# A linear-attention and feed-forward kernel: the engines' order written by hand, and the weights loaded in order through one queue

## The chip, the cores and the metric

The kernel runs on one core of one Trainium2 chip. The metric is device time in microseconds (us) of one execution. Each number called a time is the median of two to eleven executions. All executions of all kernels here were in the fast state, on several chips of the same kind, so each variant is set against executions of the kernel before on the same chip, in the same rounds. A ratio is the mean time of one kernel's fast runs over the mean time of the other's fast runs of the same rounds, so it is not quite the ratio of the medians that are quoted.

The profile covers one execution. It measures a span, which is a little shorter than the time; the profiled execution of the kernel before has a span of 220.7 us.

Engines: PE is TensorE (matmul), PEld its weight loads, DVE is VectorE, ACT is ScalarE, POOL is GpSimd, SP is SyncE, which here only issues transfers (SPq in the profile).

## The reference

Two layers follow each other. The first is a linear attention with a decay `f` per channel, with 4 batches, 8 heads, 768 tokens and a head width of 48. The second is a feed-forward network with a leaky ReLU, from 384 to 2048 and back, over all 3072 tokens.

```python
f = 1.0 / (1.0 + np.exp(-f_logit))
for t in range(S):
    state = f[:, :, t, :, None] * state + einsum('bhd,bhe->bhde', k[:, :, t], v[:, :, t])
    y[:, :, t] = einsum('bhd,bhde->bhe', q[:, :, t], state)
x = y.transpose(0, 2, 1, 3).reshape(B * S, H * D)     # 3072 x 384
h = x @ w_in                                          # 384 -> 2048
out = np.maximum(0.01 * h, h) @ w_out                 # 2048 -> 384
```

Inputs and outputs are float32. Both kernels compute the products in bf16.

## The kernel before

The work is cut into 24 units: 6 chunks of 128 tokens for each of 4 batches. The four batches of a chunk come first, then the next chunk. A unit has an attention part and a feed-forward (FFN) part, and the FFN of a unit stands two units behind its attention in the source. The order of the instructions on each engine is not that of the source: a scheduler in the compiler chooses it.

Attention of one unit has these steps, with the tile names that the profile shows. Four loads bring `f_raw`, `q`, `k` (both into `qk_raw`) and `v_raw`. ACT makes `t_e` and `lf` (the logarithm of the decay). TensorE sums it over the tokens (`cs`), ACT takes two exponentials of that (`ex`), and DVE multiplies q and k with them (`qkh`, the decay product). TensorE transposes (`tp`), DVE copies (`qkT`), TensorE multiplies k with q on 64 rows (`pw`), DVE masks (`wm`), TensorE forms the output (`py`), DVE copies it (`xnat`), and a DMA transposes it (`xT`). On the side, `pt`, `a_e`, `a_d`, `st`, `sf` and `sb` carry the state to the next chunk.

```python
    inp = ctx.enter_context(tc.tile_pool(name="inp", bufs=4))
    ...
    def load_weights():
        for kk in range(3):
            nc.gpsimd.dma_start(out=w_in_b[:, kk, :],          # float32 to bf16 on the way
                                in_=moe_w_in[kk * 128:(kk + 1) * 128, :])
        for kk in range(4):
            nc.gpsimd.dma_start(out=w_out_b[:, 4 * kk:4 * kk + 4, :], in_=moe_w_out[...])

    def attn(u):
        ...
        nc.sync.dma_start(out=f_raw, in_=f_logit[b, :, ts, :].rearrange("h t d -> t h d"))
        ...                                                    # q, k, v in the same way
        if u == 0:
            load_weights()
        nc.scalar.activation(t_e, f_raw, AF.Exp, scale=-1.0)
        nc.scalar.activation(lf[:, :, 0:D], t_e, AF.Ln, bias=1.0)
        nc.gpsimd.tensor_copy(out=v_b, in_=v_raw)
        nc.tensor.matmul(cs, ut, lf[:, :, 0:D], start=True, stop=True)
        nc.scalar.activation(ex[:, 0:H, :], cs, AF.Exp, scale=-1.0)
        nc.scalar.activation(ex[:, H:2 * H, :], cs, AF.Exp, scale=1.0)
        nc.vector.tensor_mul(qkh[:, :, 0:D], qk_raw, ex)
        ...                                                    # tp, qkT, pw, wm, py, xnat
        nc.sync.dma_start_transpose(xT, xnat)
        ...                                                    # state for the next chunk
        return xT

    def ffn(u, xT):
        for g in range(4):                                     # 4 x 12 up products
            for j in range(4):
                for kk in range(3):
                    mm(pm[:, j, :], w_in_b[:, kk, ...], xT[:, kk, :], 3 * j + kk, 12)
            nc.scalar.activation(gT[:, 4 * g:4 * g + 4, :], pm, AF.Prelu, alpha=0.01)
        for ff in range(16):                                   # 16 down products
            mm(po, gT[:, ff, :], w_out_b[:, ff, :], ff, 16)
        nc.vector.tensor_copy(out=osb, in_=po)
        nc.sync.dma_start(out=out[...], in_=osb)

    waiting = []
    for u in range(NU):
        waiting.append((u, attn(u)))
        if len(waiting) > DEPTH:                               # DEPTH = 2
            ffn(*waiting.pop(0))
```

## Time and profile before

| | before |
|---|---|
| time, median of 3 | 221.88 us (221.37 to 223.13) |
| span of the profiled execution | 220.7 us |
| first up product of unit 0 | 36.04 us |
| first transposes of neighbouring units, steady | 7.575 us apart |

First come the span, the busy times and the row of TensorE on the page of the kernel before. Each digit of the row is the busy share of one fortieth of the span, in tenths.

```profile
span 220.7 us, 5773 instructions
...
PE 178.7 (81%) x2376; PEld 135.4 (61%) x2376; DVE 105.5 (48%) x149; ACT 98.7 (45%) x213; POOL 50.0 (23%) x100
...
PE   0000045999798989999999999999999999999993
```

TensorE is busy 81% of the span. The row shows where the rest is: at five and a half microseconds per digit, the first seven are empty or half empty. This is why the share of the whole span should not be read as a property of the steady part. The table of stretches separates the two. Its columns are the stretch, its length, the busy time and count of PE, PEld, DVE, ACT and POOL, the granted clock, the share of the DMA engines, and GB/s. The DMA share sums the time of packets in flight and can pass 1.

```profile
0.00:10.00 10.00, 0.48 (x1) 0.10 (x1) 0.83 (x9) 2.33 (x3) 5.88 (x16) 1.00 0.83 153
10.00:20.00 10.00, 0.00 (x0) 0.00 (x0) 0.00 (x0) 0.00 (x0) 0.00 (x0) 1.00 1.20 187
20.00:30.00 10.00, 1.64 (x16) 1.11 (x16) 1.65 (x2) 2.74 (x6) 1.01 (x2) 1.00 1.11 197
30.00:40.00 10.00, 5.34 (x62) 4.46 (x63) 4.70 (x7) 3.65 (x9) 4.22 (x8) 1.00 1.02 201
...
100.00:120.00 20.00, 19.64 (x268) 15.06 (x266) 11.13 (x17) 10.30 (x24) 4.22 (x10) 1.00 0.66 144
```

In the first 40 us TensorE works 7.5 us (0.48 + 0.00 + 1.64 + 5.34), and the DMA engines are full all along. In 100 to 120 us TensorE is busy 19.64 of 20 us. A reader could conclude that nothing is to be gained there. The chain of waits says otherwise. Its columns are start, duration and what ran, and the rows are those of one round in the steady part.

```profile
107.06 1.95 PE po L89 x12
109.01 0.18 PE cs L115
...
109.21 0.49 ACT ex L117
109.70 0.38 ACT ex L118
110.08 0.50 ACT gT L188
...
110.62 0.49 PE pm L89 x6
...
111.13 0.62 PE tp L89 x8
```

The records of matmuls overlap: that of an up product is 220 ns long in the mean on this kernel's page, while up products start 56 ns apart where nothing waits. So a TensorE that reads as busy can be one whose next instruction waits. On this chain a round leaves TensorE: `cs` releases the two `ex`, they hold up `gT` on ACT, and only then do the last 6 up products run. Three ACT instructions, 0.49 + 0.38 + 0.50 = 1.4 us, stand on the chain of nearly every steady round. Not all of that is lost, since TensorE works on meanwhile. The distance between matmul starts shows how much is: in the round from 111.13 us on, the step to the last 6 up products is 329 ns where up products otherwise start 56 ns apart, the step from an up product to the first transpose is 230 ns in place of 56, and the step from a down product to the `py` that needs the mask is 275 ns in place of 162. Together that is 0.27 + 0.17 + 0.11 = 0.56 us of waiting in the round.

Three rows of the timeline show the start of the same kernel. Columns are start, duration, engine, line, operation, tiles and shapes, and in brackets the idle time before with what ended it.

```profile
23.40 0.50 POOL L112 CAST v_b<-v_raw 128x384 bf16<-128x384 f32 x1 [16.95 <-DMA v_raw<-in_v_dram]
...
25.20 0.52 ACT L109 ACTIVATE t_e<-f_raw 128x384 f32<-128x384 f32 x1 [20.51 <-DMA f_raw<-in_f_logit_dram]
...
36.04 0.80 PE L89 MATMUL pm<-xT,w_in_b 128*128 128x128 bf16 x6 [1.63 <-DMA xT<-xnat]
```

Unit 0's `v` has landed only at 23.4 us, and unit 1's `f` at 25.2 us, though all the loads were issued from 0.74 us on. The weights, loaded on POOL's queue, shared the DMA engines with them.

### The profile page before, as it was taken

To read this page: it belongs to the slowest core of one execution; us is meant where nothing else is said; L and a number is where in the kernel's file an instruction comes from. 1 tells how busy PE (TensorE), PEld (TensorE's weight loads), DVE (VectorE), ACT (ScalarE), POOL (GpSimd) and SP (SyncE) were. 2 spreads that over 40 slices of the span, in tenths; PEclk is the share of its full clock that TensorE was granted. 3 is DMA by queue.
4 is the path that set the end of the run, shared out by engine and by line. 5 is a ranking of instruction groups with operands and counts; after the bars stand their busy time and mean duration, and the time that the engine had idled before them with its cause. 6 is when DMAs were issued, how large, how long until landed. Compare 5 with 4: busy or idle time off the path is not lost.

```text
span 220.7 us, 5773 instructions
## 1 busy us (share of the span) xinstructions
PE 178.7 (81%) x2376; PEld 135.4 (61%) x2376; DVE 105.5 (48%) x149; ACT 98.7 (45%) x213; POOL 50.0 (23%) x100
## 2 busy tenths in 40 slices
PE   0000045999798989999999999999999999999993
PEld 0000034777576777777778777767777777767771
DVE  1000144765655755574566467555745666356211
ACT  4000324753744665474556446553744462535440
POOL 8100115433203303321331133033213300000000
PEclk9999999999999999999999999999999999999999
DMA  6999999578979797986766675554724411011200
GB/s 112 203 186 184 199 198 201 109 147 179 215 165 198 173 197 155 229 179 151 160 142 150 139 146 125 120 134 80 157 61 88 110 53 56 18 39 53 56 36 36
DMA packets 115850, 29.46 MB, mean 133 GB/s; under 512 B 110321, under 2 KB 115441, under 8 KB 115825
## 3 DMA queue, kind: packets, MB, share of 16 engines
q1 hardware_dynamic: 113280, 25.96, 55.9%
q0 software_dynamic: 2544, 3.15, 8.3%
q8 instruction: 18, 0.29, 0.6%
q14 instruction: 8, 0.06, 0.1%
HBM read 25.17 MB, written 4.72 MB: 135 GB/s over the span
## 4 chain that ended last, share of the span: by engine, by line
PE 63%; ACT 14%; SPq 12%; DMA 6%; DVE 2%; issue 2%; DVEq 0%; ACTq 0%
PE po L89 26%; PE pm L89 18%; PE tp L89 6%; PE py L89 5%; ACT gT L188 5%; ACT ex L117 4%; DMA f_raw<-in_f_logit_dram 4%; SPq L101 4%; PE pw L89 3%; ACT ex L118 3%; SPq L98 3%; SPq L99 3%; SPq L100 3%; PE pt L89 2%; DVE wm L134 2%
## 5 line engine op out<-in xcount | busy, mean ns | idle before, releaser
L89 PE MATMUL pm<-xT,w_in_b 128*128 128x128 bf16 x1152 | 80.4, 220 | 6.6 <-ACT gT L188 3.0
L89 PEld LDWEIGHTS <-w_in_b 128*128 128x128 bf16 x1152 | 68.8, 98 | 14.8 <-issue 11.6
L89 PE MATMUL po<-w_out_b,gT 128*128 128x384 bf16 x384 | 69.9, 326 | 0.0
L188 ACT ACTIVATE gT<-pm 128x512 bf16<-128x512 f32 x96 | 56.4, 597 | 19.3 <-PE pm L89 17.8
L89 PEld LDWEIGHTS <-gT 128*128 128x128 bf16 x384 | 34.9, 97 | 19.1
L117 ACT ACTIVATE ex<-cs 128x384 bf16<-128x384 f32 x24 | 11.7, 490 | 47.1 <-PE cs L115 47.1
L193 DVE COPY osb<-po 128x384 f32<-128x384 f32 x24 | 13.4, 557 | 39.8 <-PE po L89 39.7
L134 DVE TENSOR_TENSOR wm<-pw,ut 128x1024 bf16<-128x1024 f32 x24 | 29.4, 1223 | 3.8 <-PE pw L89 3.1
L109 ACT ACTIVATE t_e<-f_raw 128x384 f32<-128x384 f32 x24 | 12.5, 522 | 33.8 <-DMA f_raw<-in_f_logit_dram 33.8
L125 DVE COPY qkT<-tp 128x1024 bf16<-128x1024 bf16 x24 | 16.6, 691 | 17.2 <-PE tp L89 17.2
L89 PE MATMUL tp<-ident,qkh_88 128*128 128x128 bf16 x64 | 5.4, 231 | 22.4 <-DVE qkh_88 L119 22.3
L112 POOL CAST v_b<-v_raw 128x384 bf16<-128x384 f32 x24 | 13.5, 561 | 40.3 <-DMA v_raw<-in_v_dram 23.0
L163 POOL TENSOR_TENSOR a_d<-a_e,half 128x8 f32<-128x8 f32 x20 | 4.0, 202 | 80.7 <-ACT a_e L161 80.7
L89 PEld LDWEIGHTS <-qkh_88 128*128 128x128 bf16 x92 | 5.5, 103 | 27.0 <-DVE qkh_88 L119 26.9
L119 DVE TENSOR_TENSOR qkh_88<-qk_raw,ex 128x768 bf16<-128x768 f32 x8 | 7.7, 956 | 27.8 <-ACT ex L118 27.8
L147 DVE CAST xnat<-py 128x384 bf16<-128x384 f32 x24 | 13.4, 557 | 11.0 <-PE py L89 10.5
L89 PEld LDWEIGHTS <-qkT 64*128 64x128 bf16 (+1 forms) x272 | 9.6, 97 | 6.5 <-DVE qkT L125 2.1
L89 PEld LDWEIGHTS <-wm 128*128 128x128 bf16 x192 | 6.6, 97 | 9.2 <-DVE wm L134 9.1
L118 ACT ACTIVATE ex<-cs 128x384 bf16<-128x384 f32 x24 | 11.7, 487 | 0.0
L89 PE MATMUL py<-v_b,wm 128*128 128x48 bf16 x192 | 9.1, 186 | 2.2 <-DVE wm L134 2.1
L119 DVE TENSOR_TENSOR qkh_92<-qk_raw,ex 128x768 bf16<-128x768 f32 x8 | 7.7, 958 | 6.5 <-ACT ex L118 6.5
L89 PE MATMUL pw<-qkT 64*128 64x128 bf16 x192 | 9.9, 226 | 0.8 <-DVE qkT L125 0.8
(60 smaller groups left out, 123.7 us busy)
## 6 DMA issues: line engine op xcount, KB each, us to landing
f_raw<-in_f_logit_dram SPq DMA_DIRECT2D x24, 192.0 KB, 3.4
qk_raw<-in_q_dram SPq DMA_DIRECT2D x24, 192.0 KB, 3.7
qk_raw<-in_k_dram SPq DMA_DIRECT2D x24, 192.0 KB, 3.9
v_raw<-in_v_dram SPq DMA_DIRECT2D x24, 192.0 KB, 3.5
out_dram<-osb SPq DMA_DIRECT2D x24, 192.0 KB, 2.1
w_in_b<-in_moe_w_in_dram POOLq DMA_DIRECT2D x3, 512.0 KB, 8.9
w_out_b<-in_moe_w_out_dram POOLq DMA_DIRECT2D x4, 384.0 KB, 16.1
xT<-xnat SPq DMA_TRANSPOSE x24, 2.8
```

The lines of the kernel that those rows point to most:

```text
L89: nc.tensor.matmul(o, l, r, start=(i == 0), stop=(i == n - 1), is_transpose=(True if tr else None))
L101: nc.sync.dma_start(out=v_raw, in_=v[b, :, ts, :].rearrange("h t d -> t h d"))
L109: nc.scalar.activation(t_e, f_raw, AF.Exp, scale=-1.0)
L112: nc.gpsimd.tensor_copy(out=v_b, in_=v_raw)
L117: nc.scalar.activation(ex[:, 0:H, :], cs, AF.Exp, scale=-1.0)
L118: nc.scalar.activation(ex[:, H:2 * H, :], cs, AF.Exp, scale=1.0)
L119: nc.vector.tensor_mul(qkh[:, :, 0:D], qk_raw, ex)
L125: nc.vector.tensor_copy(out=qkT, in_=tp)
L134: nc.vector.tensor_mul(wm, pw.rearrange("a r p t -> a (r p) t"), ut[:, None, :].to_broadcast([128, 2 * NP, 128]))
L147: nc.vector.tensor_copy(out=xnat, in_=py.rearrange("a h d -> a (h d)"))
L188: nc.scalar.activation(gT[:, 4 * g:4 * g + 4, :], pm, AF.Prelu, alpha=0.01)
L193: nc.vector.tensor_copy(out=osb, in_=po)
```

## The change

The intent is twofold. In the steady part every engine gets its order by hand, so that independent TensorE work stands between each producer and its consumer. At the start the loads arrive in the order in which they are needed. Four things change together:

- The source is turned into a loop over rounds in the order of the engines, and `manual_schedule` makes the compiler keep it. In one round the attention of unit i is interleaved with quarters of the FFN of unit i-2 and with the preparation of unit i+1.
- The weights are loaded as float32 quarters through SP's queue, behind and between the first units' loads, and POOL casts them.
- Units 0 and 1 are turned by TensorE (three transposes and a copy) instead of a DMA.
- `inp` gets a fifth buffer. `sb` is doubled, which the new order needs: a round writes the new state before it reads the old one.

```diff
-    inp = ctx.enter_context(tc.tile_pool(name="inp", bufs=4))
+    inp = ctx.enter_context(tc.tile_pool(name="inp", bufs=5))
...
-        sb = const.tile([128, NP, 2 * D], BF16, tag=f"sb{b}", name=f"sb{b}")
+        sb = [const.tile([128, NP, 2 * D], BF16, tag=f"sb{b}{i}", name=f"sb{b}{i}")
+              for i in range(2)]
...
-    def load_weights():                    # 7 casting loads on POOL's queue
...
+    def load_w_in(g):
+        t = wst.tile([128, 3, 512], FP32, tag=f"wi{g}", name=f"wi{g}")
+        nc.sync.dma_start(out=t, in_=w_in_v[:, :, 512 * g:512 * g + 512])
+        staged["i", g] = t
+    def cast_w_in(g):
+        nc.gpsimd.tensor_copy(out=w_in_b[:, :, 512 * g:512 * g + 512], in_=staged["i", g])
...                                         # load_w_out, cast_w_out in the same way
-        nc.sync.dma_start_transpose(xT, xnat)
+            if self.u < LAG:               # LAG = 2
+                for i in range(3):
+                    mm(tx[:, i, :], xnat[:, 128 * i:128 * i + 128], ident, i, 3, tr=True)
+                nc.vector.tensor_copy(out=self.xT, in_=tx)
+            else:
+                nc.sync.dma_start_transpose(self.xT, xnat)
...
-    waiting = []
-    for u in range(NU):
-        waiting.append((u, attn(u)))
-        if len(waiting) > DEPTH:
-            ffn(*waiting.pop(0))
-    for w in waiting:
-        ffn(*w)
+    ctx.enter_context(tc.manual_schedule())
...
+    units[0].load()
+    for g in range(4):
+        load_w_in(g)
+    units[1].load()
+    load_w_out(0)
+    load_w_out(1)
+    units[2].load()
+    load_w_out(2)
+    load_w_out(3)
+    units[0].prep()                        # t_e, lf, v_b
+    units[0].cumsum()                      # cs, ex
+    units[0].decay()                       # qkh
+    for g in range(4):
+        cast_w_in(g)
+    for i in range(NU + LAG):
+        a, n, m = unit(i), unit(i + 1), unit(i - LAG)
+        unit(i + 3).load()
+        m.up(0)
+        m.up(1)
+        a.transposes()                     # tp, qkT
+        a.update_state()                   # pt, a_e, a_d, st, sf, sb
+        n.prep()
+        if i == 1:
+            for g in range(4):
+                cast_w_out(g)
+        m.down(0)
+        m.up(2)
+        a.scores()                         # pw, py with the state, wm
+        m.down(1)
+        m.up(3)
+        n.cumsum()
+        a.outputs()                        # py with wm, xnat, xT
+        n.decay()
+        m.down(2)
+        m.down(3)
+        m.store()
```

## The prediction

> **What bounds the kernel now.**
>
> *Start.* In the table of stretches TensorE is busy 0.5, 0.0, 1.6 and 5.3 us in the first four 10 us, with the DMA engines at least 83% busy. The timeline shows why: the weights (casting loads on POOL's queue) share the 16 DMA engines with the first units' loads; v_raw of unit 0 lands at 23.4 us, unit 1's f_raw at 25.2. Unit 0's first up product runs at 36.0. That all queues run on the same 16 engines and interleave is what the Trainium skill says (DMA: Bandwidth & Descriptors, "Issuing engines are not separate DMA queues"); this trace agrees.
>
> *Steady state.* From 80 to 200 us TensorE is busy 97.8%; the first transpose of successive units comes every 7.575 us (88.40, 95.98, 103.55 in the chain of waits). But that busy time holds pipeline latency. The chain has 18 up products in 1.00 us (56 ns each) and 12 down products in 1.95 us (162 ns). 48 up (2.67) + 16 down (2.59) + 8 transposes (0.45) + cs 0.16 + pw 0.21 + py and state 0.37 + pt 0.27 make 6.7 us, with 0.12 at the change from the 64-row pw 6.85. So about 0.6 us per unit is wait: the chain passes through ACT (ex, ex, gT: 1.4 us per unit) before the last up products and the decay product, then qkT to pw, and wm to py.
>
> **What the change does.** Between cs and the next unit's transposes stand py, two down and two up quarters (2.9 us of TensorE), against 2.7 us for gT, ex, ex and decay (0.97 us): just hidden. qkT (0.69) hides behind pt, down and up (1.6), wm (1.22) behind down, up and cs (1.5). I expect 7.0 us per round (6.75 without pt in four), 5.3 in the two rounds without attention.
>
> Weights: fp32 through SP's queue, in order. 192-byte packets take 15.9 ns (mean of the records), so a unit's 4096 packets take 4.1 us on 16 engines. A weight quarter, estimated from the 65 ns of the 1536-byte output packets: 2.1 us. So unit 0 lands at 6.5 us, w_in at 15, unit 1 at 19, unit 2 at 27.5, w_out at 32, unit 3's f at 33. Added: eight POOL casts, estimated 2.0 us each from 503 ns per 384 columns. The w_out casts stand behind the cast of unit 2's v, end near 36 us and gate round 2, which ends at 36.7. Unit 2's DMA transpose stands behind the loads of units 4 and 5 (some 1 us).
>
> **Sum.** 36.7 + 17 x 7.0 + 4 x 6.75 + 2 x 5.3 + 1 + 3.4 (last product to end, as before) = 198; timed runs lie 1.2 us above the span: 199 us. Some 14 of the 23 us gained come from the start.
>
> Chances: faster by over 2% 0.96, within 2% 0.03, slower 0.01. Range 194 to 206.
>
> **What would show it.** First transposes every 7.0 us; no large ACT releaser before up products; TensorE near full from 37 us, with waits before that for POOL's w_out casts and f_raw; first up product near 27 us.
>
> **What would make it wrong.** Slower weight packets or POOL casts (10% is 2 us); an order on ACT or DVE that keeps a wait in each round (0.2 us is 4 us in all); a backlog on SP's queue that delays every transpose.

## The result and the profile after

| | before | after |
|---|---|---|
| time, median (4 runs each, same rounds) | 221.84 us | 201.17 us (200.44 to 201.67) |
| ratio, 95% interval | | 0.9057 (0.9009 to 0.9105) |
| span of the profiled execution | 220.7 us | 198.7 us |
| first up product of unit 0 / unit 8 / unit 23 | 36.04 / 101.43 / 211.63 us | 28.42 / 87.32 / 189.30 us |
| distance of the first transposes of neighbouring units, steady | 7.575 us | 6.967 us |

The changed kernel is faster by 9.4%. All outputs are right. The page of the kernel after has these busy times and this row of TensorE:

```profile
span 198.7 us, 5720 instructions
...
PE 171.8 (86%) x2382; PEld 137.4 (69%) x2382; DVE 106.1 (53%) x151; ACT 103.4 (52%) x213; POOL 55.8 (28%) x101
...
PE   0401449898999999999999999999999999999992
```

The table of stretches of the kernel after, for the same stretches:

```profile
0.00:10.00 10.00, 2.53 (x25) 1.91 (x26) 3.36 (x13) 3.37 (x6) 2.23 (x10) 1.00 0.82 211
10.00:20.00 10.00, 1.10 (x12) 0.73 (x11) 1.38 (x2) 1.92 (x4) 7.37 (x7) 1.00 0.99 284
20.00:30.00 10.00, 4.93 (x53) 4.17 (x52) 5.51 (x8) 2.15 (x6) 3.72 (x6) 1.00 1.06 298
30.00:40.00 10.00, 9.37 (x129) 7.49 (x127) 6.32 (x9) 5.61 (x13) 7.32 (x9) 1.00 1.02 235
...
100.00:120.00 20.00, 20.00 (x291) 16.12 (x287) 12.77 (x18) 12.56 (x27) 5.64 (x12) 1.00 0.73 154
```

In the first 40 us TensorE now works 17.9 us (2.53 + 1.10 + 4.93 + 9.37) instead of 7.5. In 100 to 120 us TensorE is busy 20.00 of 20 us. This time it is real: from 46 to 183 us no two matmuls start more than 0.17 us apart, and the longest steps are those behind 384-column products (0.16 us) and at `pw` (0.15 us). One round on the chain of waits:

```profile
106.72 0.16 PE cs L131
106.88 0.20 PE py L100 x8
107.08 1.30 PE po L100 x8
108.38 1.34 PE pm L100 x24
109.72 0.45 PE tp L100 x8
```

The chain now stays on TensorE. `cs`, `py`, 8 down products, 24 up products and the transposes follow each other at the pace of their starts (the 24 up products take 1.34 us, 56 ns each), with no ACT row between them. The start, in rows of the timeline that answer to those before, with some that are used further down:

```profile
6.26 1.10 POOL L127 CAST v_b<-v_raw 128x384 bf16<-128x384 f32 x1 [4.57 <-DMA v_raw<-in_v_dram]
...
28.42 2.56 PE L100 MATMUL pm<-xT,w_in_b 128*128 128x128 bf16 x24
...
28.94 2.11 DVE L138 TENSOR_TENSOR qkh_96<-qk_raw,ex 128x768 bf16<-128x768 f32 x1
...
30.18 2.19 POOL L97 CAST w_out_b<-wo_142 128x1536 bf16<-128x1536 f32 x1
...
34.45 0.53 ACT L124 ACTIVATE t_e<-f_raw 128x384 f32<-128x384 f32 x1 [2.27 <-DMA f_raw<-in_f_logit_dram]
...
35.58 0.32 PE L131 MATMUL cs<-lf_87,ut 128*128 128x384 bf16 x1 [0.51 <-ACT lf_87 L125]
```

Unit 0's `v` is cast at 6.26 us instead of 23.40, and the first up product starts at 28.42 us instead of 36.04. One wait in the steady part was left, the one for the first transpose by DMA, that of unit 2:

```profile
41.31 2.73 SPq L208 DMA_TRANSPOSE xT<-xnat  x1
...
45.51 1.51 PE L100 MATMUL pm<-xT,w_in_b 128*128 128x128 bf16 x24 [1.17 <-DMA xT<-xnat]
```

SP issues it at 41.31 us, and the up products that need it start at 45.51 us, after TensorE has waited 1.17 us.

### The profile page after: what moved, and what is told of

The parts are those of the page before. It is cut to its first block, busy times and chain, and to the rows that moved or that the text cites. A ratio compares the mean times of both kernels' runs of the same rounds, so it can differ in the third digit from the quotient of the medians.

```text
span 198.7 us, 5720 instructions
## 1 busy us (share of the span) xinstructions
PE 171.8 (86%) x2382; PEld 137.4 (69%) x2382; DVE 106.1 (53%) x151; ACT 103.4 (52%) x213; POOL 55.8 (28%) x101
## 4 chain that ended last, share of the span: by engine, by line
PE 78%; SPq 13%; DMA 6%; ACT 1%; issue 1%; DVE 0%; ACTq 0%
PE po L100 30%; PE pm L100 30%; SPq L120 10%; PE py L100 5%; PE tp L100 5%; DMA f_raw<-in_f_logit_dram 4%; PE pw L100 3%; PE pt L100 2%; DMA xT<-xnat 2%; PE cs L131 2%; SPq L85 1%; SPq L90 1%; ACT gT L219 0%; DVE osb L230 0%; ACT t_e L124 0%
## 5 line engine op out<-in xcount | busy, mean ns | idle before, releaser
L219 ACT ACTIVATE gT<-pm 128x512 bf16<-128x512 f32 x96 | 57.2, 597 | 64.3 <-PE pm L100 60.2
L100 PEld LDWEIGHTS <-w_in_b 128*128 128x128 bf16 x1152 | 71.3, 99 | 10.6 <-DMA xT<-xnat 1.6
L100 PE MATMUL pm<-xT,w_in_b 128*128 128x128 bf16 x1152 | 77.1, 221 | 1.2 <-DMA xT<-xnat 1.2
L100 PE MATMUL po<-w_out_b,gT 128*128 128x384 bf16 x384 | 74.5, 325 | 0.2
L100 PEld LDWEIGHTS <-gT 128*128 128x128 bf16 x384 | 32.4, 97 | 17.0 <-ACT gT L219 1.5
L100 PEld LDWEIGHTS <-wm 128*128 128x128 bf16 x192 | 8.6, 98 | 13.7 <-issue 11.8
L127 POOL CAST v_b<-v_raw 128x384 bf16<-128x384 f32 x24 | 12.7, 532 | 16.5 <-DMA v_raw<-in_v_dram 14.2
L138 DVE TENSOR_TENSOR qkh_88<-qk_raw,ex 128x768 bf16<-128x768 f32 x8 | 7.9, 993 | 7.7 <-ACT ex L134 7.7
L138 DVE TENSOR_TENSOR qkh_96<-qk_raw,ex 128x768 bf16<-128x768 f32 x8 | 8.8, 1102 | 3.3 <-ACT ex L134 3.3
L131 PE MATMUL cs<-lf_91,ut 128*128 128x384 bf16 x8 | 2.8, 345 | 8.8 <-ACT lf_91 L125 8.8
L138 DVE TENSOR_TENSOR qkh_92<-qk_raw,ex 128x768 bf16<-128x768 f32 x8 | 7.7, 956 | 3.3 <-ACT ex L134 3.3
```

Source lines behind the costliest of these rows:

```text
L100: nc.tensor.matmul(o, l, r, start=(i == 0), stop=(i == n - 1), is_transpose=(True if tr else None))
L127: nc.gpsimd.tensor_copy(out=self.v_b, in_=self.v_raw)
L138: nc.vector.tensor_mul(self.qkh[:, :, 0:D], self.qk_raw, self.ex)
L219: nc.scalar.activation(self.gT[:, 4 * g:4 * g + 4, :], pm, AF.Prelu, alpha=0.01)
```

## The experiments

The theory of the prediction is that the change gains about 14 us at the start, through the order of loads and weights, and about 0.6 us in each later round, because the order on TensorE hides the waits. Its rivals are: the weights alone do nearly all; the source order alone does it and the compiler's scheduler would find the same with it; any fixed order would do, since the scheduler is the culprit; or the fifth input buffer does it. Eleven kernels were run. Four of them (any fixed order, quarters undone, the cumulative sum at the end, units 0 and 1 turned by DMA) had one round of two executions, the others three or five rounds.

### The order alone

The kernel after with the weight loads of the kernel before.

```diff
     units[0].load()
-    for g in range(4):
-        load_w_in(g)
+    ...  # the 7 casting loads of before, on POOL's queue
     units[1].load()
-    load_w_out(0); load_w_out(1)
     units[2].load()
-    load_w_out(2); load_w_out(3)
...
-    for g in range(4): cast_w_in(g)        # and cast_w_out(g) in round 1
```

> The changed kernel with the weight loads put back as they were before: seven casting loads issued from POOL's queue right behind unit 0's loads, no fp32 staging, no POOL casts. Theory (start and steady state are two separate gains): the steady round stays at 6.97 us from transpose to transpose, but unit 0's v lands at about 23 us instead of 6, the first transposes come at about 27 us, the first up product at about 37 instead of 28.4; 206 to 209 us in all. Rival (the hand order alone makes the gain, the weights are hidden anyway): 201 us.

Measured: 205.09 us against 221.30, ratio 0.9257 (0.9227 to 0.9287), a little below the range of 206 to 209 us that was expected. The rounds are 6.97 us, as in the kernel after. Unit 0's first up product starts at 34.41 us, 6.0 us later than in the kernel after and only 1.6 us earlier than in the kernel before. "Order" stands here for all that is not the weights: the turning of units 0 and 1 by TensorE, the early loads of units 1 and 2 and the fifth buffer are in this variant too.

### The weights alone

The kernel before, scheduler and all, with the float32 quarters on SP's queue and the casts on POOL.

```diff
         if u == 0:
-            load_weights()
+            for g in range(4):
+                load_w_in(g)               # load, then nc.gpsimd.tensor_copy
+        if u in (1, 2):
+            load_w_out(2 * u - 2)
+            load_w_out(2 * u - 1)
```

> The kernel before with only the weight loads changed to those of the changed kernel (fp32 quarters in SP's queue between the loads of units 0, 1 and 2, cast on POOL); source order and pools as before. Theory: unit 0's transposes at about 7 us, the start gains 8 to 12 us, the steady round stays at 7.58 us; 210 to 214 us in all. Rival (the start was bound by the order, not by the weights): 219 to 222 us.

Measured: 216.72 us against 221.30, ratio 0.9779 (0.974 to 0.9817), so a gain that is clear of zero, but about which the 2% verdict is unclear. It is less than the 210 to 214 us of the expectation: the early start came, but not the time. The first up product starts at 17.59 us, which is 18.5 us before that of the kernel before and 10.8 us before that of the kernel after. The rounds are again 7.57 us where nothing else waits. TensorE has long pauses in the early units, and its granted clock falls to 0.89, 0.84 and 0.93 in the three stretches from 20 to 50 us.

The two halves add up. The order alone takes off 7.4%, the weights alone 2.2%, together 9.6%, and the change takes off 9.4%. But they do not fall where the prediction had them, as this table of first up products shows (us, in brackets the lead on the kernel before):

| | unit 0 | unit 8 | unit 23 |
|---|---|---|---|
| before | 36.04 | 101.43 | 211.63 |
| order alone | 34.41 (1.6) | 91.45 (10.0) | 193.44 (18.2) |
| weights alone | 17.59 (18.5) | 93.60 (7.8) | 205.53 (6.1) |
| after | 28.42 (7.6) | 87.32 (14.1) | 189.30 (22.3) |

The weights give a lead of 18 us that is given back: 6 us are left at unit 23. A part of the loss is made by the casts themselves: between 25 and 39 us TensorE waits 4.4 us in four pieces for casts of `w_out`, the last two of which stand behind unit 2's state work on POOL and start only at 35.79 us. So it is not only the order on TensorE that spends this lead. The order gives a lead that grows all the way, with 10 us of it already in the first eight units, where the kernel before took 65.4 us for eight units (8.2 us each).

### The scheduler back in

The kernel after without its line `tc.manual_schedule()`, so with the new source order as a mere suggestion.

```diff
-    ctx.enter_context(tc.manual_schedule())
```

> The changed kernel with the one line that fixes the order by hand taken out, so that the scheduler may reorder again; the source is written in the new order. Theory A (the order in which the source calls the pieces makes the gain; the scheduler mostly keeps it): 201 us, steady round 6.97 us. Theory B (the scheduler's own choices cost the time before, so it gives the gain back): round of 7.3 to 7.6 us, 208 to 213 us.

Measured: 215.35 us against 221.30, ratio 0.9719 (0.9674 to 0.9765). That is theory B in kind, and beyond its range of 208 to 213 us. More than two thirds of the gain are lost (2.8% against 9.4%), though the instructions are the same in kind and number. The timeline of TensorE shows how the scheduler used its freedom:

```profile
12.87 2.72 PE L100 MATMUL pm<-xT,w_in_b 128*128 128x128 bf16 x24 [0.45 <-DVE xT L206]
...
45.16 0.61 PE L100 MATMUL tp<-ident,qkh 128*128 128x128 bf16 x8
...
50.24 0.62 PE L100 MATMUL tp<-ident,qkh 128*128 128x128 bf16 x8 [1.52 <-DVE qkh L138]
...
54.97 1.04 PE L100 MATMUL tp<-ident,qkh 128*128 128x128 bf16 x8 [0.89 <-DVE qkh L138]
55.80 2.76 PE L100 MATMUL pm<-xT,w_in_b 128*128 128x128 bf16 x24
```

It starts the FFN of unit 0 at 12.87 us, more than 15 us before the hand-written order. But then it puts the attention of units 3, 4 and 5 (their transposes at 45.16, 50.24 and 54.97 us) ahead of unit 2's first up product at 55.80 us, for which the hand-written order needs only 45.51 us. That attention waits for itself at each step. TensorE also falls back to its slow clock in these pauses: eight transposes at 54.97 us take 1.04 us instead of 0.61, and 24 up products 2.76 us instead of 1.51. Against the kernel after, this one is 10.3 us behind at unit 2 (55.80 less 45.51) and 14.4 us behind at unit 23 (203.74 less 189.30). Where rounds run undisturbed they take 6.97 us here too, so the scheduler often finds an order as good. Between 77 and 125 us, however, some rounds last up to 9.0 us, because ACT waits for late `f_raw` loads. Why those loads come late there was not settled.

The Trainium skill describes the clock in "TensorE: Matmul & The Clock Gate", Part 1: TensorE starts at half clock and returns to it after about 3.4 us without work, with 107 ns between 128-column matmuls cold and 56 ns warm. This case agrees with the two paces, but not with the pause: in the variant just shown the transposes at 50.24 us still start 56 ns apart and those at 54.97 us start 106 to 107 ns apart after the first step, and the longest idle stretch of TensorE between 45 and 55 us is 1.52 us. A row of shorter pauses was enough here. In the kernel after, unit 0's first 24 up products start 106.7 ns apart (20 of the 23 gaps), the next at 56 ns. The row of the granted clock on the page shows nothing of this short stretch: it has a 9 in all its digits.

### Any fixed order

The kernel before with its source order held fixed: attention of one unit from end to end, then an FFN from end to end.

```diff
+    ctx.enter_context(tc.manual_schedule())
     waiting = []
```

> The kernel before with its order fixed to that of its source, as the changed kernel does with its own: a unit's attention from end to end, then the FFN of the unit two before, nothing interleaved. It tells how much of the hiding the scheduler had already done. Theory (the scheduler had interleaved all but 0.6 us of each round; without it about 4.6 us of attention chain per round stand open): round of 11 to 12.5 us, 285 to 330 us in all. Rival (pipelining over units is enough, the scheduler's order was the cost): under 222 us.

Measured: 480.32 us, ratio 2.17, far above what was expected. The rounds take 19.3 us. The timeline shows the part that the expectation had not counted:

```profile
212.49 0.36 SPq L194 DMA_DIRECT2D out_dram<-osb  x1
212.95 0.39 SPq L98 DMA_DIRECT2D f_raw<-in_f_logit_dram  x1
...
215.96 0.52 ACT L109 ACTIVATE t_e<-f_raw 128x384 f32<-128x384 f32 x1 [6.06 <-DMA f_raw<-in_f_logit_dram]
```

The order of SP is fixed as well. The load of the next `f_raw` (212.95 us) stands behind the store of the last FFN (212.49 us), so nothing is loaded ahead, and ACT waits 6.06 us for it. TensorE then idles so long that the granted clock is 0.72 of full speed in the mean, and the 48 up products of an FFN take 3.7 to 5.0 us (all but the last two FFNs) instead of 2.7. So a fixed order alone does not help, and a scheduler does much of the hiding. The source order, held fixed, costs the kernel before 259 us (480.32 less 221.32). A fixed order is only as good as its order.

### Quarters undone

The kernel after, with the four up quarters in one block before the attention and the four down quarters in one block behind it.

```diff
-        m.up(0); m.up(1)
+        for g in range(4): m.up(g)
         a.transposes(); a.update_state(); n.prep()
-        m.down(0); m.up(2)
         a.scores()
-        m.down(1); m.up(3)
         n.cumsum(); a.outputs(); n.decay()
-        m.down(2); m.down(3)
+        for g in range(4): m.down(g)
```

> The changed kernel with the interleaving by quarters undone: in each round all four up quarters, then the attention pieces one behind the other, then all four down quarters. Same work, same weights, same hand-made pipeline over units. Theory (the quarters hide qkT, wm and lf from TensorE): TensorE waits about 0.7 us for qkT, 1.15 for wm and 0.15 before the third up quarter in each round; round of about 8.9 us, 240 to 248 us in all, slower than the kernel before. Rival (the other engines are only half busy, so their slack absorbs it; the gain is in pipelining over units): 201 to 206 us.

Measured: 245.08 us, ratio 1.1019 (1.0928 to 1.1111), rounds of 8.79 us, as expected. Without the quarters the hand-written order is slower than the kernel before. The new waits are where the attention is left alone:

```profile
107.40 0.40 PE L100 MATMUL pw<-qkT 64*128 64x128 bf16 x8 [0.54 <-DVE qkT L145]
...
109.12 0.37 PE L100 MATMUL py<-v_b,wm 128*128 128x48 bf16 x8 [0.65 <-DVE wm L190]
```

The first row is `pw`, which waits for the copy `qkT`, the second is `py`, which waits for the mask `wm`. The profile counts an idle stretch only from the end of the last result. Counted from start to start, and less what the same step costs without a wait, a round has 0.58 us more from `pt` to `pw` (0.70 less 0.03 for a `pt` product and 0.10 for the change to 64 rows), 0.81 us from `cs` to `py` (0.97 less 0.16), 0.26 us from `py` to `cs` (0.28 less 0.03) and 0.18 us before the third up quarter (0.23 less 0.06). Together that is 1.83 us, and a round is longer by 1.82 us (8.79 less 6.97).

### The cumulative sum at the end

The kernel after, with `cs` and the decay product behind the last two down quarters, so that only two up quarters hide them.

```diff
         a.scores(); m.down(1); m.up(3)
-        n.cumsum()
         a.outputs()
-        n.decay()
         m.down(2); m.down(3)
+        n.cumsum()
+        n.decay()
```

> The changed kernel with one piece moved: the cumulative sum of the next unit (and its decay product) comes after the two last down quarters instead of before py. Theory (the order just hides the chain cs, ex, ex, decay product, about 2.3 us from cs to the first transpose, behind py and four quarters; now only two up quarters, 1.5 us, are left): TensorE waits about 0.8 us before the transposes of each round, round of about 7.75 us, 216 to 219 us in all. Rival (there is slack to spare on ACT and DVE): 201 us, round of 6.97.

Measured: 217.36 us against 221.94, ratio 0.9773 (0.9692 to 0.9854; at 2% against the kernel before unclear, but clearly slower than the kernel after with 0.9057), rounds of 7.77 us against an expected 7.75.

```profile
100.14 1.50 PE L100 MATMUL pm<-xT,w_in_b 128*128 128x128 bf16 x24
102.25 0.62 PE L100 MATMUL tp<-ident,qkh 128*128 128x128 bf16 x8 [0.62 <-DVE qkh L138]
```

The 24 up products start 0.17 us behind `cs` (99.97 us) and at 56 ns each have all started by 101.5 us, but the transposes start at 102.25 us, 2.28 us after `cs`, because the chain `cs`, `ex`, `ex`, decay product takes that long. So the place of one matmul is worth 0.8 us per round, more than the whole difference between the rounds of before and after. So the chain that stood in every round of the kernel before comes back as a wait of TensorE as soon as too little work stands behind `cs`, and the place of `cs` in the new order is what hides it. From `cs` to the first transpose the kernel before has 2.12 us (109.01 to 111.13), this one 2.28, and the kernel after 3.00 (106.72 to 109.72), because there it has that much other work to do.

### The fifth buffer

```diff
-    inp = ctx.enter_context(tc.tile_pool(name="inp", bufs=5))
+    inp = ctx.enter_context(tc.tile_pool(name="inp", bufs=4))
```

> The changed kernel with four input buffers, as before, in place of five. Theory (a round's loads go to the buffer of the unit before last, whose readers are long done, so the fifth buffer hides nothing): 201 us, within 0.5%. Rival (loads are held back at the head of each round): 203 us or more, with waits for f_raw.

Measured: 201.10 us, ratio 0.9077 (0.9038 to 0.9116), as the kernel after (0.9057). The fifth buffer does nothing that shows.

### Units 0 and 1 turned by DMA

```diff
-            if self.u < LAG:
+            if False:
```

> The changed kernel with units 0 and 1 transposed by DMA like all others. Theory (a DMA transpose of unit 0 is issued behind unit 3's loads on SP's queue and lands behind them, near 37 us): first up product near 37 us instead of 28.4, 207 to 211 us in all. Rival (the two TensorE transposes do not matter): 201 us.

Measured: 208.16 us, ratio 0.936 (0.9285 to 0.9434), so 6.7 us of the gain (3.0% of 221.94) hang on this small branch.

```profile
34.91 1.28 SPq L208 DMA_TRANSPOSE xT<-xnat  x1
...
38.11 2.72 PE L100 MATMUL pm<-xT,w_in_b 128*128 128x128 bf16 x24 [10.24 <-DMA xT<-xnat]
```

SP's order is fixed, and the first transpose stands behind all the loads issued before it. It is issued only at 34.91 us, and TensorE waits 10.24 us until 38.11 us. A fixed order on a queue that loads also use needs a way around that queue while it is full.

### The loads behind the transpose

The remaining wait, 1.17 us for unit 2's transpose, was put down to the loads of units 4 and 5 ahead of it on SP's queue. From round 2 on, the round's loads are moved behind its transpose.

```diff
-        unit(i + 3).load()
+        if i < 2: unit(i + 3).load()
...
         a.outputs()
+        if i >= 2: unit(i + 3).load()
```

> The changed kernel, but from round 2 on a round's four loads are issued after the transpose of that round, not at the head of the round. Theory (unit 2's DMA transpose landed at 45.5 us because it stood behind two units' loads in the queue, and TensorE waited 1.2 us for it): the wait before the first up product of unit 2 goes, 1.0 to 1.3 us less, 199.9 to 200.2 us; the steady round is unchanged. Rival (the transpose is late for a cause of its own, or the loads, now later, stop the rounds): 201 us or more.

Measured: 199.46 us against 221.30, ratio 0.9007 (0.8978 to 0.9036). Unit 2's first up product starts at 44.15 us instead of 45.51, without a wait. The 1.36 us gained at this place are about the half per cent by which the ratio is lower than that of the kernel after (0.9057), and the time is a little below the 199.9 to 200.2 us that were expected. The intervals of the two ratios overlap, so it is the trace and not the time that shows this gain.

### The FFN half a unit earlier

Two attempts built on the last one. The FFN runs one and a half units behind the attention instead of two, so that TensorE has FFN work earlier and the end is shorter, and units 0 to 2 are turned by TensorE.

```diff
-        m.up(0); m.up(1)                   # m is unit i-2 all round
+        down(i - 2, 1); up(i - 2, 3)
         a.transposes(); a.update_state(); n.prep()
-        m.down(0); m.up(2)
+        down(i - 2, 2); down(i - 2, 3); unit(i - 2).store()
         a.scores()
-        m.down(1); m.up(3)
+        up(i - 1, 0, 1)
         n.cumsum(); a.outputs()
+        unit(i + 3).load()
         n.decay()
-        m.down(2); m.down(3)
+        down(i - 1, 0); up(i - 1, 2)       # rounds 0 to 3 are written out apart
```

> A version meant to beat both: loads behind the transpose (as in e4_loads_later), and the stream of up and down quarters moved half a unit earlier against attention (unit 0's up quarters already in round 1, where TensorE waits for loads; up 0 and 1 of the unit before last round's stand beside cs, down 0 and up 2 after py); unit 2 also transposed by TensorE. Theory (TensorE is the limit from 37 us on and idle before, so what moves into the first 30 us is gained in whole, half a unit's 5.3 us): round 6.97 us, last round shorter, 196.5 to 197.5 us. Rival (the start is bound by what has landed, so nothing fits in earlier): 199.5 us or more.

Measured: 199.59 us, ratio 0.8989 (0.8937 to 0.9041). That is at least 2 us more than was expected, and no better than the version above. The timeline named the causes: TensorE waited 2.15 and 0.24 us for casts of `w_out`, the second half of which stood behind the state work of unit 2 on POOL and ended only at 38.2 us, and 1.01 us for the copy of an output. The second attempt moves the last two casts ahead of that state work and spreads unit 0's and unit 1's down products differently in rounds 2 and 3.

```diff
         a.transposes()
+        if i == 2: cast_w_out(2); cast_w_out(3)
         a.update_state()
-        if i == 2: cast_w_out(2); cast_w_out(3)
```

> e7_shifted with its two faults in round 2 mended: POOL casts the last two w_out quarters before unit 2's state work (they had landed by 34 us but were cast from 35.3 to 38.2, and TensorE waited 2.4 us), and unit 0's last down quarter and its copy stand before cs, so that the next down quarter does not wait for the copy (1.0 us). Theory: unit 3's transposes at 38.7 to 39.5 us instead of 41.5, everything behind it moves by the same; 196.5 to 197.7 us. Rival (what has landed is the limit): 199 us or more.

Measured: 196.78 us (196.00 to 197.19, 6 runs) against 221.32, ratio 0.8879 (0.8846 to 0.8913). This is the best version, ahead of both kernels.

```profile
35.45 0.81 PE L100 MATMUL po<-w_out_b,gT 128*128 128x384 bf16 x4 [0.90 <-POOL w_out_b L97]
...
39.21 0.62 PE L100 MATMUL tp<-ident,qkh 128*128 128x128 bf16 x8
```

Of the waits, 0.90 us for a cast and 0.29 us for a copy are left, and unit 3's first transpose starts at 39.21 us instead of the 41.52 of the first attempt. The rounds are 6.967 us, as in the kernel after, so what is gained lies outside the steady rounds.

## Why the prediction was right, and where not

**The time.** 199 us was predicted with a range of 194 to 206, and 201.17 was measured.

**What bounded the kernel before: right.** The chain through ACT was named as the loss of the steady part, about 0.6 us per round. The round went from 7.575 to 6.967 us, which is 0.61 us, with the same matmuls. The three long steps of the round before (329, 230 and 275 ns) are 56, 56 and 163 ns in the kernel after, which is 0.56 us of the 0.61. The experiment with `cs` at the end put a wait for the same chain back, at a size that the chain's durations give.

**The round after: right, with one term too small.** 7.0 us was predicted and 6.967 measured. The sum had 0.12 us for the change of the 64-row `pw`. From start to start, the step into `pw` takes 152 ns and the step out of it 148 ns, where a step of this kind takes 56 ns otherwise; so 96 and 92 ns, 0.19 us per round, also where `qkT` had long been ready (ready at 55.16 us, `pw` at 55.96). The Trainium skill, in "TensorEngine Tiling (Array Packing)", Key Properties, says that a switch of the tiling mode drains TensorE. The trace agrees and adds the size.

**The sum.** The terms of the prediction against the trace:

| term | predicted us | measured us |
|---|---|---|
| end of round 2, from zero | 36.7 | 37.4 |
| 17 rounds | 119.0 | 118.4 |
| wait for unit 2's DMA transpose | 1 | 1.2 |
| 4 rounds without state | 27.0 | 26.6 |
| 2 rounds without attention | 10.6 | 11.6 |
| last product to end of span | 3.4 | 3.5 |
| span | 198 | 198.7 |
| time above span | 1.2 | 1.7 |

The largest error of a term is the 1.0 us of the last two rounds. There TensorE waits for `gT` twice in each, because no attention stands between the quarters any more: the step to the first down quarter is 238 and 297 ns in place of 56, and a step to the last one 364 ns in place of 162, which is 0.8 us in the two rounds. The time above the span had been taken from one execution's span and another's time, which is not allowed: within one execution it is 1.79 us before (222.49 less 220.7) and 1.74 after. The table ends at the profiled execution of 200.44 us. The median of the four, 201.17, lies 0.7 us above it, and no term stands for that.

**The start: the total right, several steps wrong.** Errors of both signs cancelled.

- "Weight quarter 2.1 us" was too little. The float32 weight packets took 95.6 ns (2048 bytes) and 75.9 ns (1536 bytes, output packets among them), not 65, so a quarter took 2.3 to 2.4 us. Unit 3's `f`, expected at 33 us, was used at 34.45 us.
- "Casts 2.0 us each", scaled from 0.50 us for 384 columns, was too much: most took 1.47 us. A linear scale charges the fixed part of an instruction four times: 0.50 us for 384 columns and 1.47 for 1536 make 0.84 ns per column and about 0.18 us that is fixed. The Trainium skill would have helped, in "GPSIMD Engine Reference", 3.1: for simple bodies 1.03 cycles per element, with a fixed dispatch beside it. At the 1.2 GHz used there, an estimate from that page is 1.32 us for 1536 columns plus the fixed part, which fits the 1.47 us of this trace. The section has larger figures for other bodies too, so this fit was found with the result in hand.
- "The w_out casts gate round 2" was wrong. They ended at 35.5 us, TensorE never waited for one, and what it waited for instead was `lf` of unit 3 (0.51 us at 35.58 us, in the rows of the start above).
- The cold clock was not counted. Unit 0's first two up quarters have a record of 2.56 us instead of 1.51. The first up product itself came at 28.42 us rather than "near 27".
- The wait for unit 2's transpose was right in place, cause and size: predicted some 1 us behind the loads of units 4 and 5, measured 1.2, and gone when those loads were moved behind it.

**The weak step: "Some 14 of the 23 us gained come from the start", in the words that put the start down to the weights.** The figure holds if the start is taken to last to unit 8, where the kernel after leads by 14.1 us; at unit 0 it leads by 7.6. As the prediction did not say where the start ends, this agreement is in part luck. The cause was mis-assigned. The prediction counted the start as the work of the loads, but the order alone already leads by 10.0 us at unit 8, and the weights alone give back two thirds of an 18 us lead. What the early weights buy is an earlier start of FFN work. That it takes an order which keeps TensorE busy afterwards to turn this into time is the reading of these runs, not isolated by one of them. Of the 20.7 us that the change gains, some 16 go with the order (205.09 us without the weights) and some 4 are added by the weights. Some 7 of the 16 need the turning of units 0 and 1 by TensorE, if the experiment on the kernel after holds for the order alone as well.

**What stays open.** The waits for late `f_raw` loads in the variant that the scheduler ordered, and why the kernel before took 8.2 us per unit over its first eight units rather than 7.6, are described but no experiment isolates them.

## What to carry to other kernels

A TensorE that reads as 98% busy can still wait in every round: look at the distance between the starts of its instructions and at which other engines stand on the chain of waits. Give each producer and its consumer a piece of independent TensorE work in between that is longer than the path between them, and cut the big products into pieces small enough to do so; one matmul in the wrong place cost 0.8 us per round here, and whole blocks instead of quarters cost 1.8. A fixed order fixes the transfer queue as well, so place loads and transposes on it as carefully as the matmuls, and test an earlier load by where the lead is at the end, not by when the first product starts.

## What the Trainium skill lacked or had wrong

- "TensorE: Matmul & The Clock Gate", "Back-to-back issue gap": it gives about 81 ns per matmul for sustained pairs of weight load and 128-column matmul, and calls 56 ns the gap of an isolated one. Here up products, each with its own 128x128 weight load, start 56 ns apart in a sustained stream (624 gaps between 80 and 175 us of the kernel after), and 384-column ones 162 ns apart.
- The same page, Part 3, "The mechanism": it says that weight loads overlap matmuls in flight only when their row groups differ, though it also names a background weight buffer. Here weight loads of all 128 rows, about 99 ns per record, run beside matmuls that start every 56 ns.
- "TensorEngine Tiling (Array Packing)", Key Properties: the drain at a switch of the tiling mode has no figure. Here it cost 96 ns into the 64-row products and 92 ns out of them.
- "GPSIMD Engine Reference", 3.1: there is no measured time of a cast from float32 to bf16. Here 128x384 took 0.50 us and 128x1536 took 1.47 us.
- "SBUF — State Buffer", "SBUF: two separate sides", states the rule, and that the later one waits for the whole of the earlier, but no time for this pair, and the prediction had not counted it: a DVE instruction with two SBUF inputs and a GpSimd instruction that reads SBUF exclude each other at a shared pair of ports. The trace agrees. In the rows of the start, the decay product at 28.94 us takes 2.11 us instead of 0.96, and the POOL cast at 30.18 us takes 2.19 us instead of 1.47. They lost 1.15 and 0.72 us; the transposes behind the decay product came 0.28 us late for it (a step of 340 ns in place of 56).
